# Masked-key copies and a transposed-x copy from ScalarE to VectorE in the prologue of an attention and mixer block

## The chip, the cores and the metric

The kernel runs on one core of one Trainium2 chip. The metric is device time in microseconds (us). A core has five engines that work side by side, each through its own list of instructions in order: TensorE (PE in the profile; its weight loads are PEld), VectorE (DVE), ScalarE (ACT), GpSimd (POOL) and SyncE (SP, which here only starts DMA transfers). They wait for each other by semaphores. Matmul results go to PSUM, eight banks of 128 partitions x 512 fp32 numbers; VectorE and ScalarE copy them from there into SBUF, where the kernel has one tensor, `arena`, for everything.

## The reference

x is 2048 rows of 640 numbers. Two branches start from its layernorm and are multiplied at the end.

```python
def _A_ref(x, wqkv, wo):                       # 32 heads of 20 numbers
    qkv = (x @ wqkv).reshape(B, S, 3, H, Dh).transpose(2, 0, 3, 1, 4)
    q, k, v = qkv[0], qkv[1], qkv[2]
    p = softmax(einsum("bhqd,bhkd->bhqk", q, k) * Dh ** -0.5)
    o = einsum("bhqk,bhkd->bhqd", p, v)
    return o.transpose(0, 2, 1, 3).reshape(B, S, D) @ wo

def _B_ref(x, w1, w2, w3, w4):
    h = gelu(layernorm(x) @ w1)
    # the four quarters of h are moved by +1, -1, +2, -2 rows: g0..g3
    x1 = x + concatenate([g0, g1, g2, g3], -1) @ w2
    return x1 + gelu(layernorm(x1) @ w3) @ w4

xn = layernorm(x)
out = x + _A_ref(xn, A_wqkv, A_wo) * silu(_B_ref(xn, B_w1, B_w2, B_w3, B_w4))
```

## The kernel before

**The work.** The 32 heads are taken in 8 groups of four (quads), and each quad in 4 chunks of 512 queries. For one chunk, 16 tiles of 128 keys are multiplied with the queries: these are the scores. ScalarE takes their exponential, 1024 columns at a time (L1692; 2048 in L1669); for some tiles VectorE does it with integer arithmetic (L1715, then L1602, or L1600 on GpSimd). TensorE multiplies the result with the values (L1432, L1614) and adds it up in bank 7. The other seven banks are a pool that scores and projections share. The mixer and MLP branch and the projections of later quads are worked on between the score tiles.

**Two forms of matmul.** Nearly all matmuls stand in groups of four that use four column strips of the array at once (L733 for projections, L1079 for transposes). Scores can use the four row strips instead (L1623), one strip for each head; a score whose neighbours on TensorE are in column form is done in column form too (L1640). Each change between the two forms takes TensorE some time.

**The prologue.** x is loaded (L920), then the weights of queries and keys of quad 0 (L1102) and of the values (L1341). Layernorm runs tile by tile. TensorE transposes x (L1079) for three of the four column blocks g (the second but one, g = 2, goes by DMA); for each block 5 tiles, numbered `bk` = 0 to 14, are copied out of PSUM, on ScalarE (L1087) where `bk` is in the list `TRA`, on VectorE (L1090) otherwise. `prep` then makes queries and keys of quad 0:

- for each chunk c the key projection (L733) goes to a bank, VectorE takes its largest absolute value (L1217, `mx_c`), and the keys are copied out with a mask and a constant, `mask * k + eaug` (L1220, `kev_c`, on ScalarE);
- the four maxima give a bound of the scores (L1232, L1234), by which the queries of each chunk are shifted: their own copy is L1156, the shift L1165 on TensorE and L1171 on VectorE;
- the first four key tiles start early with a bound from chunk 0 alone (L1186, L1192, L1196), and L1204 and L1208 (`fe`) make the factor by which their sum is corrected later (L1408).

Scores of key tiles 4c to 4c+3 need `kev_c`. A bank comes free when its copy has ended.

**What sets the order.** The functions only record tasks: engine, what is read and written, which bank pool. The string `TABLE` holds the order of all tasks and the bank that each takes; `Planner.follow` reads it and adds the waits that data and banks need. So each engine's order is written out, and nothing is decided at run time. `AGAIN` lists scores that are multiplied more than once (quad, chunk, key tile, head: how many times more), with the same result.

Of the kernel before, what the change touches and what calls it, by code (L numbers as in the profile page):

```python
# [457 lines left out]
U8 = mybir.dt.uint8  # L458
# [19 lines left out]
class Cfg:  # L478
# [5 lines left out]
    def __init__(self, S=2048, D=640, H=32, F=1536):  # L484
# [61 lines left out]
        self.TRA = [1, 2, 4, 5, 6, 7, 8, 9, 13, 16]  # L546
# [110 lines left out]
class Gen:  # L657
# [447 lines left out]
    def prep(self):  # L1105
# [104 lines left out]
        for c in range(NQC):  # L1210
            if c == 1:
# [7 lines left out]
                   reads=[wa], writes=[A("MXc", c)], name=f"mx_{c}", due=self.at(0, "mx", 1, "mxs", c))  # L1219
            T("act", c_act(512) + 100, lambda e, h=h, c=c: e.activation(KT[:, 0, 512 * c:512 * c + 512], self.wbank(h)[:, 0:512], AF.Identity,  # L1220
# [921 lines left out]
    r"#6#9#%#,###(#-#$#&#'#.#e#w&R#l$S#)#*#+#2#Z#f#g$K#[#n$L#]#^$J#h#`#m#c#_#/&S#:#;#<#=#>#?#@#A#B#C#D#E#F#G#H#I#J#K#L#M$M#i#o#p#j#q$'#k${##N#O#P#Q%$$#R#S$q&#T$N#r"  # L2142
    r"$O#s#{$`#x$P#|#y#t$Q#}#z$T$U$V$R$W#b$|#a#d%%&Q#v#~#u$}%&%'$X$##U$l($m$n$v%$r$s$t$w$x$y$~#V$o#W#X#Y$8$)%($u$($z$a$Y$$$*$Z%#$p%g$%`#%a$,$[$]$+$^$_$6#5$-$4%n$%$"
    r"D$5$&$.$/%p$9%b%c$b%h%i%j%8'%k&j&%d&k%9%:%)%&[)&]%l%e$:&^&_%*&`%+%;%3($7$2$3&a$A%<%4%5%6%,&l%=#%>%?&m%.)&T'%7%/$C%@&n%f%0%q$;%1&U&V&c(&W%-&d&e&f&X%2%A&g%r%%t"
    r"#&w)%C$0$@&o$B%u%v%w&x&y&Y$c$E%s$1$<$?$F$>&h&z%m&{*?#$d*<)&|*;(*@$*A%%x'(($G')*='%B'*$e$='+',&6)&7*9#*8$$f$I$g*:&$h'-&8&9&}($H*5(*4)&~*6(%E%D&:'#**#*+$'$'%$i"
    r"$j%U%$k*,$%y%F$%V%G%H%W%o&;%K)%z(H*>%L'&%M%P(%Q%N%I%Z&%O%[%X%R%]%^%{'%|%S%J%}*C)%T%Y*B(%_*2&*1'%~&#(I&&(&'&(&)&<&*'d*D)*-(*3&&$&+*.)*/'&-#0';&'<'=&.'>'?&H#&I"
    r"&2)&J&K(G(J&/&L*7*0&,'@&3&%*]&*^%*_$*J$*K#*H(&M*I)*L&&?#&@&A&B*M&C&4(&5*Q$*P#+#)+$(&D+%'*N&*O'*E'/('0*S'1'2*F'3*U#*V$*R)&q$&=%&r(P&s*W#*X&'4*Y%&>&t&u*f$&v+/("
    r"*Z%+.'*g#*T'I$'J*`%'e#4*G+P(L(K+0(*i*a&'K'L'M''*[*}#'N*|$*m(*l)*o*b&&p*j&*k'&i'5(*~)'6'7'8'9*n#':+1$+2#+3%*c+&+?&*d)&E*r+@'*e('B('C'D'E'F'U&'V'W*h&'X'Y+9$'G+"
    r"A'+8%+:)#7+*(++)+4'O#'P'Q'R'S'.'A&N'H*p+,%*{*x+5%+6&+T$'Z+S#+7#'T*t']#+')*u+((+V'^'_'`'a+Z%+F$+G#+Y&+)&*s'b+;+H(+]+C''c+D(&F$+-+R#+i&+h%+E#+Q$*z+U%&G,#)+~(&O"
    r"#*y+k+I,%#,$)+o&+n%&P+q+t,&$*q'f#+W(+X),'#'g'h+<#+=$,@%,A&'i+[('j'l$'m'k*v+>$*w+B,B&+`(+_',2#,3$+J,5+a$,~'n+c%+b&'o+^&Z'p+l'+d'+m(,(,1#,0$'q+K,9&+p%,8%'r$,;'"  # L2150
    r"s+f'+g('t,4#'u,=#,>$,6&+j)+z,7%'v2d+e,?('w'x#'y+},N(,M),E#,D$'z'{+w'|,P,:$,k%,l&+v,T(,F),S),H#,G$'},<(M#,m%,e&,V'~'[,d%(N,I'+r,C-1(,f$-0',g#,h$,i&,J+s-2)+x+u"
    r",X-&&(#&0-%%,r#,,),s$+|+y,j,-(,t#+{-(,W,Q%,R&,],)#,*$(%#(&('(((),.',+$,^,n(,U&-,#-+$,Y(O,o),p(,[(*,/,v',u&,w$(+((,(--.-:(-9),K#,L$+L,O'(.,q(Q-$&-#'-'%,`+M(/-"
# [128 lines left out]
```

## Time and profile before

| | us |
|---|---|
| runs | 789.10, 789.43, 791.61 |
| median | 789.43 |
| profiled execution, its own time | 788.74 |
| span of the profiled execution (first to last instruction) | 787.0 |
| ScalarE busy in the span | 765.8 |
| TensorE busy, as modelled | 772.6 |
| VectorE busy | 682.0 |
| GpSimd busy | 440.1 |

The granted TensorE clock was 0.999 over the span. Times in the views count from the first instruction. In a group's line stand the source line, the engine, the operation, what it writes and reads, how often, then its busy time and the mean of one in ns, and the idle time of its engine just before with what ended most of it. In a timeline a row is its start, its length, and equal instructions merged; the bracket is the idle time in front and what ended it. `x28` for TensorE is 28 instructions, that is 7 groups of four. Matmuls are pipelined, so a matmul's row is longer than the time from one to the next.

### The profile page before, as it was taken

The page shows a single profiled execution, that of the slowest core. Times are in us where ns is not written, and L with a number is a line of the kernel's source. Part 1 is how long each engine was busy: PE and PEld are TensorE (multiplying, and loading weights), DVE is VectorE, ACT ScalarE, POOL GpSimd, SP SyncE. Part 2 cuts the span into 40 slices and gives each one's busy share as a digit, 9 for nine tenths or more (in the row PEclk, how much of TensorE's full clock was granted, in tenths as well). Part 3 has the DMA queues.
Part 4 walks back from the last instruction along what each step waited for, and adds up shares of the span by engine and source line. Part 5 has one row for each costly group of instructions (what it writes and reads, how often), then busy time and mean ns, then how long its engine had stood idle before and what let it go on. Part 6 is the DMA issues. An engine that isn't in the chain of part 4 may idle for free.

```text
span 787.0 us, 27583 instructions
## 1 busy us (share of the span) xinstructions
PE 772.6 (98%) x12412; PEld 289.8 (37%) x12412; DVE 682.0 (87%) x906; ACT 765.8 (97%) x803; POOL 440.1 (56%) x238
## 2 busy tenths in 40 slices
PE   9999999999999999999999999999999999999997
PEld 5433323324444322333423333323334333332554
DVE  8888888988899989987988889888989879896886
ACT  7999999999999999999999999999999999999996
POOL 6575656553457546666555654676444455636742
PEclk9999999999999999999999999999999999999999
DMA  6403542342122223443221161233341113113443
GB/s 176 88 15 84 136 130 70 88 106 45 14 63 53 49 63 70 98 75 69 53 69 53 36 119 37 61 79 62 73 107 44 19 36 92 21 17 102 134 134 109
DMA packets 141349, 58.09 MB, mean 74 GB/s; under 512 B 113728, under 2 KB 136432, under 8 KB 141232
## 3 DMA queue, kind: packets, MB, share of 16 engines
q1 hardware_dynamic: 141232, 56.33, 31.0%
q8 instruction: 97, 1.59, 0.8%
q14 instruction: 20, 0.16, 0.1%
HBM read 34.70 MB, written 10.33 MB: 57 GB/s over the span
## 4 chain that ended last, share of the span: by engine, by line
PE 51%; ACT 47%; DVE 1%; issue 0%
ACT arena L1692 40%; PE psum L733 19%; PE psum L1623 15%; PE psum L1614 8%; PE psum L1432 6%; ACT arena L2098 3%; PE psum L907 1%; ACT arena L1669 1%; ACT arena L2006 1%; PE psum L1640 1%; ACT arena L2126 1%; PE psum L1489 1%; ACT L1692 0%; DVE arena L1715 0%; PE psum L1463 0%; PE psum L1079 0%
## 5 line engine op out<-in xcount | busy, mean ns | idle before, releaser
L1692 ACT ACTIVATE arena<-psum 128x1024 bf16<-128x1024 f32 x730 | 678.6, 1092 | 10.0 <-PE psum L1623 6.1
L1600 POOL TENSOR_TENSOR arena<-arena 128x2048 int32<-128x2048 int32 x92 | 330.2, 3599 | 198.3 <-DVE arena L1602 122.5
L1715 DVE TENSOR_SCALAR arena<-psum 128x1024 uint16<-128x1024 f32 x264 | 321.4, 1220 | 61.0 <-PE psum L1623 57.0
L733 PE MATMUL psum<-arena 128*32 128x320 bf16 (+1 forms) x5808 | 330.6, 333 | 0.1
L1623 PE MATMUL psum<-arena 32*128 32x512 bf16 x1930 | 257.1, 384 | 5.5 <-ACT arena L1692 3.0
L1614 PE MATMUL psum<-arena 128*22 128x512 bf16 x2112 | 182.0, 381 | 0.0
L733 PEld LDWEIGHTS psum<-arena 128*32 128x32 bf16 x5808 | 134.2, 96 | 122.5 <-issue 52.7
L1623 PEld LDWEIGHTS psum<-arena 32*128 32x128 bf16 x1930 | 69.7, 91 | 232.2 <-ACT arena L1692 151.7
L1432 PE MATMUL psum<-arena 128*22 128x512 bf16 x1456 | 139.2, 382 | 0.6 <-ACT arena L1692 0.5
L1602 DVE TENSOR_SCALAR arena<-arena 128x4096 uint16<-128x4096 uint16 (+1 forms) x121 | 130.1, 1089 | 4.2 <-PE psum L1614 3.4
L1749 POOL TENSOR_TENSOR arena<-arena 128x512 bf16<-128x512 f32 x30 | 40.6, 1355 | 52.0 <-DVE arena L1602 40.5
L1614 PEld LDWEIGHTS psum<-arena 128*22 128x22 bf16 x2112 | 46.9, 90 | 57.6 <-issue 38.6
L1432 PEld LDWEIGHTS psum<-arena 128*22 128x22 bf16 x1456 | 35.1, 90 | 47.7 <-issue 32.0
L2091 DVE CAST arena<-psum 128x512 bf16<-128x512 f32 x48 | 32.6, 683 | 5.0 <-PE psum L733 4.9
L1299 DVE CAST arena<-psum 128x512 bf16<-128x512 f32 x40 | 27.2, 683 | 3.9 <-PE psum L733 3.7
L1914 POOL TENSOR_TENSOR arena<-arena 128x640 bf16<-128x640 bf16 x12 | 16.7, 1398 | 20.7 <-DVE arena L1848 7.9
L1640 PE MATMUL psum<-arena 128*32 128x512 bf16 x272 | 26.8, 382 | 0.1
L1669 ACT ACTIVATE arena<-psum 128x2048 bf16<-128x2048 f32 x13 | 25.3, 1944 | 0.6 <-PE psum L1623 0.5
L944 DVE BATCH_NORM_STATS2 arena<-arena 128x6 f32<-128x320 bf16 x54 | 24.5, 477 | 1.4 <-DMA arena<-in_A_x_dram 1.2
L1848 DVE SCALAR_TENSOR_TENSOR arena<-psum,arena 128x320 bf16<-128x320 f32 x32 | 15.5, 488 | 8.5 <-PE psum L733 8.1
L1736 DVE STREAM_TRANSPOSE arena<-psum 128x512 f32<-128x512 f32 x30 | 21.2, 707 | 1.2 <-PE psum L1432 0.5
L961 POOL TENSOR_SCALAR arena<-arena 128x640 bf16<-128x640 bf16 x16 | 14.0, 876 | 14.5 <-DVE arena L1602 13.3
(135 smaller groups left out, 336.0 us busy)
## 6 DMA issues: line engine op xcount, KB each, us to landing
arena<-in_B_w_dram SPq DMA_DIRECT2D x48, 160.0 KB, 2.7
arena<-arena SPq DMA_DIRECT2D x124, 32.0 KB, 1.9
arena<-in_B_w_dram SPq DMA_DIRECT2D x4, 960.0 KB, 5.8
arena<-in_A_x_dram SPq DMA_DIRECT2D x8, 320.0 KB, 5.4
arena<-in_A_x_dram SPq DMA_DIRECT2D x16, 160.0 KB, 2.6
out_dram<-arena SPq DMA_DIRECT2D x16, 160.0 KB, 2.1
heads<-arena SPq DMA_DIRECT2D x120, 20.0 KB, 2.0
arena<-keys SPq DMA_DIRECT2D x28, 80.0 KB
```

The source lines that it names most:

```text
L733: ins = e.matmul(pb[32 * c:32 * c + 32, 0:N], lhsT(k, c), rhs(k, c), start=(k == 0), stop=(stop and k == nk - 1), tile_position=(0, 32 * c))
L1432: ins = e.matmul(pb[32 * i:32 * i + 22, 0:512], VA[:, ql, kts[i // 2], i, :], PT[:, slots[i // 2][0].slot, slots[i // 2][0].at(i % 2):slot ...
L1600: return e.tensor_tensor(dst.bitcast(I32), U[:, ub, 0:w].bitcast(I32), bass.AP(c.tensor, c.offset, [list(c.ap[0]), [0, w // 2]]), op=ALU.add)
L1602: fa if onp else lambda e, v=v, dst=dst: e.tensor_scalar(dst, U[:, ub, 0:w], EXP_B[v], None, op0=ALU.add),
L1614: ins = e.matmul(pb[32 * i:32 * i + 22, 0:512], wv, dst[:, at:at + 512].bitcast(BF16), start=first, stop=final, tile_position=(0, 32 * i))
L1623: return e.matmul(out, self.KT[32 * i:32 * i + 32, b, 128 * kt:128 * kt + 128], q, start=True, stop=True, tile_position=(32 * i, 0))
L1640: ins = e.matmul(out[32 * c:32 * c + 32, :], self.KT[:, b, 128 * kt + 32 * c:128 * kt + 32 * c + 32], self.QM[:, gb, i, :], start=True, st ...
L1669: lambda e: e.activation(self.PT[:, hp[0].slot:hp[0].slot + 2, :], self.psum[:, 512 * h0.slot:512 * h0.slot + 2048].rearrange("p (a b) -> ...
L1692: lambda e: e.activation(self.PT[:, hp.slot, :].rearrange("p (a b) -> p a b", b=512), self.banks(hs), AF.Exp, scale=cfg.scale),
L1715: return e.tensor_scalar(U[:, ub, 1024 * at:1024 * at + 1024].rearrange("p (a b) -> p a b", b=512), self.banks(hd), a_exp, EXP_BIAS, op0=A ...
L1749: return e.tensor_tensor(OnT.rearrange("p (k d a) -> p a k d", k=4, a=4), Ob[:, :].rearrange("p (a k d) -> p a k d", a=4, k=4), in1, op=AL ...
L2091: T("dve", c_dve(512), lambda e, h=h, fc=fc, i=i, G=G: e.tensor_copy(G[:, i, fc, :], self.wbank(h)[:, 0:512]), reads=[wa], writes=at, name ...
```

## The change

Chunks 1, 2 and 3 of the masked keys are copied by VectorE, in one `tensor_scalar` from the same bank with the same two numbers per partition. Two entries leave `TRA`: 13, the tile of block 3 with kc = 3, which VectorE then copies (L1090), and 16. `AGAIN` is a different list of about the same length. `TABLE` is new as a whole: order and banks were searched again for this set of tasks. The set itself is the same otherwise.

```diff
-        self.TRA = [1, 2, 4, 5, 6, 7, 8, 9, 13, 16]
+        self.TRA = [1, 2, 4, 5, 6, 7, 8, 9]
...
-        self.AGAIN = {(3, 3, 14, 2): 1, (7, 1, 5, 0): 1, (7, 1, 6, 0): 1, (7, 1, 7, 0): 3, (7, 1, 9, 0): 1, (7, 1, 9, 1): 1, (7, 1, 12, 0): 1, (7, 2, 6, 2): 1, (7, 2, 6, 3): 4}
+        self.AGAIN = {(2, 0, 4, 0): 1, (7, 1, 0, 3): 1, (7, 1, 4, 2): 3, (7, 1, 6, 1): 1, (7, 1, 9, 1): 1, (7, 1, 12, 0): 4, (7, 1, 14, 1): 1, (7, 1, 15, 0): 1, (7, 1, 15, 1): 1, (7, 2, 6, 2): 1}
         self.EARLY = 4
+        self.KD = (1, 2, 3)
...
             t1 = T("dve", c_dve(512), lambda e, h=h, c=c: e.tensor_reduce(MXc[:, c:c + 1], ...), ..., name=f"mx_{c}")
+            if c in cfg.KD:
+                T("dve", c_dve(512), lambda e, h=h, c=c: e.tensor_scalar(KT[:, 0, 512 * c:512 * c + 512], self.wbank(h)[:, 0:512], mask[:, 0:1],
+                                                                         self.eaug[:, 0:1], op0=ALU.mult, op1=ALU.add),
+                  reads=[wa, A("eaug"), A("maskh"), A("MXc", c)], writes=at, name=f"kev_{c}", rel=h)
+                continue
             T("act", c_act(512) + 100, lambda e, h=h, c=c: e.activation(KT[:, 0, 512 * c:512 * c + 512], self.wbank(h)[:, 0:512], AF.Identity,
                                                                         bias=self.eaug[:, 0:1], scale=mask[:, 0:1]), ..., name=f"kev_{c}", rel=h)
...
 TABLE = ( ... )    # every line differs
```

On the queues, the first loads now go x (six of eight), query weights, x, x, value weights, key weights; before they went x (five), key weights, x (three), query weights, value weights. Of the 782 tasks that stay on ScalarE, 713 keep their place in its order.

More of the change, by code (lines that the diff above doesn't have):

```diff
@@ L2145 @@
[L2145 to L2152, printed above, removed]
@@ new lines @@
+    r"%$6$@$.$a$^$_%e%3$$/$8$A%='%)#%*%+%,%-%>%?%@%4%5%A%8&%9%:%.%$5%/%0%1%;&c(&d%6&j#&k&e%2%<%f$2$9$7%l%7$3$:$0%q$;$1$C$`&f$4$<&T'&U&V&g$B&h$?&l&W&X%r&&m&n&[$&w%&"
+    r"x&y&Y&]%s&o$E$>&z&{&^&6(&_&`&7$F&a&|$G$b%m*@#$c$d%C$=%B%E%D(P$e*;'*?$*A%*<&$f$H&8&9&:%t$'(%%u%v')'*'+*4$$g*5#(H&;$h%w%x',$I$i%y'-%z*=&*6)*9&$j$k*8%&}#*+$**#*"
+    r":$&~'#'$'%'&%K(%L%Z)%[%M%U%%V%F$%G%H%W%]*,#&<&p#5%^&Z%X%N%_%Y%P#%Q%I%R%S%{&%O%J%|%}%~&#*B&*C%%T';$&&%&'%p#0&(&)&*&H#(G%o'<'='>'?*.$&$&%(I&+&-*D'*1&'@&.*2%*-#"
+    r"*>&I&2$*3(&J&K*/$&L*7&,'d&3*I&*H%*^#*K(&M*]$*J)&?#&@*L)&A&B*M&C*_(&4)*Q(*P)+#%+$$*0*E&5*O&&D*N'*S+%&'/&'0*U$*X(*R#*F*Y)*V%'1'2'3'.''&=)&q#&r&s&t&u'4&>*T*W%*Z"
@@ new lines @@
+    r"'+.#+/$&v+0#*f&*g%*i*a'*`(*[*b%'I$'J'K'L'M(J&/*}$*|#*l%'N*m&*~)*j(*k''5$'6*n$*G'7'8'9+2#*o+1$':+&'B(*e&&E+?)+3'*d'+@('C'D'E'F'U&'V&N'W'X'Y*r'G+4+9$+A&*h)+8%+"
+    r"*(++)*c'O#'P'Q+:''e&i#4'H*x'A*u'R'S*p*{'Z+,%+6$+5#'T+P+S%+T&+V']#'^+')+((+7(+)$'_'`'a*t+G$+F#+H#'b+Y&+Z%+]*s&F#+C)+D(+E)(K+-&G*q+h#+R&+i$#7+k+Q%+;&O#&P,#(+~)"
+    r"+U%,$'+I*y+n%+o&,%#,&$,'$*z'f#+q+t+X(+W)'g+[('h+<#+=$,@%,A&'c'i*v2d'j*w+z+>)'l$,B#'m'k+B+_(+`',3#,2$+J,5'n+a)+b&+c%+d&'o'p+^+m'+l(,1$,0#,9%,8&+p%'q'r$'s+e+g'"
+    r",;+f(+r,4('t+j),~(L+K,=#,7%,6&,>$'u'v+},?&'x#'y'z,E(+L'w,N#,M$,D),('{'|,P,:%,k%'},l&,F),H(,S#,T$,V(Q'~,G),m$+w+M&0,<+v,I'+s,d',h%,e&+|+u,C,g$,J,f%-1#,r)-&&,s"
@@ new lines @@
+    r"(-%'+x(#-(,i&,t',X+y-0$-2),j(M(,,(,-)+{(N,Q',Y,],R&,.&,*%,)$,W(%&(&('(((),+#,Z-,(,o$(*-+),n%,/,U(,^,u&,v'(+&(,(-,p%,w#-.,K$-:(-9),L%,q(.-#&-$''[+N-<(/,O&,x-@"
+    r"%-?$,`(O.K-'%->)-=(,[,c-Y&(Y-A$(0-Z'-B,_,a-[#,b-*)-)(--(-7$-8#(1((2(7#-E(3(4(5-K-4(-3)(8,y-/-;&(6-a$-`#-W&-c-V%-H(9(:-5'-X%-o)-n(-p((;-N(<-R%-f#-g$-S&-i-6-C-"
+    r"T$-e(-d)(Z#([-h&-k&-l%-m)-|#-{$(](^(_-s)/u-r(-t'-~-G-](`(v(=(S&-O$(o-P%.%'.&&-u(#8(R-Q#(h-v).((T(U-F-L-U-w%-^$.|'-_%.}&-b$(V(W-I.+-J-q.~#-y(.$%-z).#$(>(X&1(@"
+    r"..-x($-})-M-j+O(a.''(w&(x(y(z.5&({.,.*,z,{(?((A.4.8$(|.1.6%.9#.:).-(B-D.;%.?).O&.@(.A$.N'.Q.0.7.<$0-&(}0./v.=%0/.C).B(.U&.T'.W.D'0001.S$.R%./.>.M(.L).d&.c'02"
@@ new lines @@
+    r".E.V(.2.Z$.P%.Y%/w&.).f.3.](.[).^).i&.j'/x/y.h%.g$(C.F.l._&.k'/z/{/|.b(.a).`.X.y$/.%.z#/-&/}#.e$/~/'(/()/0.{)0#0$/%#/)&/<&/$$/;%0%/#0'$.o0&0(0)0*0+/=(/2%/1&/"
+    r"`'/_(.m.x,|,}/&)/*(~&/5#)#0,)$/,$/+%04)%/3&/a$/4'/8(//&/9)/:'.q/6.p/@$/?%)&.G/7/b()'/O&/A%/N'/c)/d)/>.r.u.s/C#/B$(b((c(F(E03/Q/D#(d/F)/I&/G(/H'/e/J'(e/M#/K05"
+    r"/L$(f(g/E/P)/i)/j(/l'/S/T/k(.v/f$/^.t/g#06$0708090:/m(/W.n.w/n&0;(D3u3x#3y$4(&.H/Z2e&b4'%40)/Y41(/X/V3{43/h/U4##4)%3~$4*&4+%4,$0<#/o3})3|(4$)0=0>0?4%0@45#0A4"
+    r"4$47%46&4.(4/)42'/R4948#/[/]0B#0C/p0D3v(3w)4<4J%4I&4K(3z&0E0F4?/q0H&5L)(.I0I4E0J4P%4Q$0K0L4-4c&4R#0G)K4b'4d$0M4V)4W(4&4T$4Y4U#(p((q(r4]&4e(4f)4X)4g&4^'4;(s4o"
@@ new lines @@
+    r"#)/)D4p$.J(t4A4`4i)(u4l&4k'4j(4=4>4h4s%5%$5&%4n4m'4q)5'$4r(4Z&4B4N#4['4@4t5$4_&4:4M$)>()?)@50(4G&4w4z)=4O%5/)4F'4D)A)B4S4C4a5(#5)$51'4H#5<(5;)4v5*)4u53&)C5>5"
+    r"4'))(4L)*55$56#57&5,(5-))+),59&5:')-5+585.#5O)5M$5P(4}5N#4x52).5=(0N5~&5Q$5}'5R/r5Z%4y4{5_#5V)5^$6#%5U(5@5`'5F4~5[&5#4|5X5A5z#5{$5](5T'5D5d(5B5e)5?(i(5S&5E(j"
+    r"9t5|)5g5C(k5b#5c$5G5k(5j)5W&62&63'5f#(l6$(m5Y5m5h$5i#66%/s6%(5l$(n5p6&)0Q5n)E#)F)G)H0V6@&6)#6($6')6A%)I0O5y5o0P$0R5a6*&6/()J69#6:$0S6.'6B$5r6+6;')L$6,%6-&)M)"
+    r"N65#6160#64$6='6<()O)P)6Da6N&6M%5q676>)5s5v5u6I'6G$6J()Q6H#6Q&6L686?6j&6K(6k%)0$)16l)6C#6O'6P(6D$)2)3)46E'6g%6R6h&6i#)55t5w5H6`$6d'6a#6c(6F6e%6U6_5x6v6X)7$6b"
@@ new lines @@
+    r"$6m)86n#)9):);)<6o'6f6S6}$6~#6W6[/t)R7%)0U6V)S$6x%6z'6y(6w&)T)U)V)W)Y)o5I0T8G6|)X76#75$6{&7R%7Q&7$(7#'6p6Y6T79#7/)71#72$)a)}6]6Z5J7&70(6^7S%)Z()[747g&73'7f'7"
+    r"8#7h(6q77$7:7@)]7V)7U()^)_7'7W&7Y$7O#7N$)`7X'7d)7P)7c(7F)b()c7Z7_$7['7^#7a7e&7]&7`#)d)e7m(7n)7o')f)h)v)g7T8.&8-'7s$8/)7t#7b7B80(81))i()j7k'7j&82#7l%)k)l7v88#"
+    r"84)87$85(7A83)m7p7;7i89$7=7r'7y#86))n8?&7z$8>%7|7?7>7q()p$)q)r8@&7w&7x%7u#8<#8;$)s)t8:8=')~#*#)u7C8#7{)7D7+(7H#7G$7,)6r7I(8&7E*$7-$*%Di))w()x)y*&)z*'){7<Dj8Q"
+    r"(8P)8`$8_#Du#)|DvDwDxDyDk8b8SDlDm5K7~Dc&Do(DzDd8K(8J)8f$DpDq2cDeDfDnDgDr8MDs6s*(3,#3-*)3.3/30Dh2f)2g2h2i2j8%2kDt318e#8'8,2{%8(7(%2m#2n2o2p8$8h7)&2t$2q2u2v2w0"
```

178 lines of the change are left out of this document (81 added, 97 removed).

## The prediction

> **What bounds the kernel now.** I read the page first: the engines' busy time, the chain that ended last, the costliest group.
>
> ```profile
> PE 772.6 (98%) x12412; PEld 289.8 (37%) x12412; DVE 682.0 (87%) x906; ACT 765.8 (97%) x803; POOL 440.1 (56%) x238
> PE 51%; ACT 47%; DVE 1%; issue 0%
> L1692 ACT ACTIVATE arena<-psum 128x1024 bf16<-128x1024 f32 x730 | 678.6, 1092 | 10.0 <-PE psum L1623 6.1
> ```
>
> ScalarE (ACT) is busy 97% of the span, nearly all of it the exponential of scores, and it sat idle before those for only 10.0 us. The chain, however, goes half through TensorE (PE). So it matters which of the two leads in the stage that the change touches. The second view is busy time by stage; the columns are the window, its length, then busy time and count of PE, PEld, DVE, ACT, POOL.
>
> ```profile
> 21.40:35.00 13.60, 13.60 (x292) 6.16 (x284) 11.56 (x29) 12.55 (x15) 7.56 (x9) 1.00 0.59 108
> 35.00:80.00 45.00, 45.00 (x653) 15.19 (x651) 39.15 (x48) 44.99 (x50) 30.43 (x24) 1.00 0.20 51
> 80.00:140.00 60.00, 59.98 (x815) 17.96 (x811) 52.66 (x60) 58.56 (x63) 35.93 (x15) 1.00 0.43 107
> 140.00:200.00 60.00, 59.41 (x943) 22.11 (x944) 52.37 (x63) 59.42 (x56) 28.76 (x12) 1.00 0.33 80
> 200.00:260.00 60.00, 59.86 (x1054) 25.33 (x1050) 55.40 (x82) 58.34 (x63) 31.18 (x14) 1.00 0.21 41
> 520.00:720.00 200.00, 197.41 (x3018) 70.55 (x3009) 170.79 (x187) 199.89 (x205) 108.27 (x38) 1.00 0.26 54
> ```
>
> From 35 to 80 us ScalarE is idle for 0.01 us: there it sets the pace. Just before, from 21.4 to 35 us, it is idle for 13.60 - 12.55 = 1.05 us. That is the stretch of the moved copies; ScalarE's timeline shows it.
>
> ```profile
> 21.39 4.69 ACT L1692 ACTIVATE arena<-psum 128x1024 bf16<-128x1024 f32 x5
> 25.94 0.80 ACT L1220 ACTIVATE arena<-psum,arena 128x512 bf16<-128x512 f32 x1
> 26.60 0.63 ACT L1087 ACTIVATE arena<-psum 128x512 bf16<-128x512 bf16 x1
> 27.77 2.98 ACT L1692 ACTIVATE arena<-psum 128x1024 bf16<-128x1024 f32 x3 [0.54 <-PE psum L1623]
> 30.64 1.44 ACT L1220 ACTIVATE arena<-psum,arena 128x512 bf16<-128x512 f32 x2
> 32.56 1.94 ACT L1692 ACTIVATE arena<-psum 128x1024 bf16<-128x1024 f32 x2 [0.48 <-PE psum L1623]
> 34.39 0.60 ACT L1208 ACTIVATE arena<-psum 128x512 f32<-128x512 f32 x1
> 35.01 5.61 ACT L1692 ACTIVATE arena<-psum 128x1024 bf16<-128x1024 f32 x6
> ```
>
> After each pair of copies ScalarE waits for TensorE's scores, 0.54 and 0.48 us. The copies stand in time that ScalarE has anyway. The chain of waits, asked for 21 to 36 us, agrees: no piece of it is on ScalarE or VectorE.
>
> ```profile
> by line: PE psum L733 59.9%; PE psum L1623 22.0%; PE psum L1079 7.9%; PE psum L1432 6.5%; PE psum L1204 2.9%; PE psum L1165 1.4%
> 27.71 1.62 PE psum L733 x28
> 31.74 0.43 PE psum L1432 x8
> 32.17 0.54 PE psum L1623 x6
> 32.71 1.19 PE psum L733 x20
> ```
>
> These rows also price TensorE's work. 28 matmuls are 7 groups of four, 20 are 5: (1.62 - 1.19) / 2 = 0.215 us for a group of 512 columns, and 1.62 - 7 x 0.215 = 0.11 us is left for the switch between row-form scores and the column form of everything else. Six scores in two passes take 0.11 + 2 x 0.215 = 0.54 us, as shown.
>
> **The change part by part.** (1) What leaves ScalarE. TRA lists tiles of transposed x by number, and only 15 exist, 0 to 14; entry 16 never named one. So one copy of x (tile 13) moves and not two, with three of keys: four instructions. In the rows above they hold ScalarE from 25.94 to 27.23 and from 30.64 to 32.08: 1.29 + 1.44 = 2.73 us. That is the most that can be gained here.
>
> (2) What TensorE must do before the first exponential after the copies' stretch (35.01 us). I counted the orders of the two built programs up to that exponential's scores: the same instructions stand there, but for one group of L1432, which goes behind. That frees 0.215 us. All else (projections, transposes, scores) is still ahead, and TensorE has no gap there. So of 2.73 us ScalarE can hand on about 0.2; the rest becomes its idle time.
>
> (3) What VectorE (DVE) gets, in its timeline:
>
> ```profile
> 26.36 1.62 DVE L1090 COPY arena<-psum 128x512 bf16<-128x512 bf16 x4 [0.48 <-PE psum L1079]
> 29.39 0.69 DVE L1217 TENSOR_REDUCE arena<-psum 128x1 f32<-128x512 f32 x1 [0.39 <-PE psum L733]
> 30.31 0.23 DVE L1234 TENSOR_SCALAR arena<-arena 128x4 bf16<-128x4 f32 x1
> 31.15 0.75 DVE L1171 SCALAR_TENSOR_TENSOR arena<-psum,arena 128x512 bf16<-128x512 f32 x1 [0.16 <-PE psum L1165]
> 31.82 0.74 DVE L1156 TENSOR_SCALAR arena<-psum,arena 128x512 bf16<-128x512 f32 x1
> ```
>
> A masked key copy has the form of L1156, and from start to start the rows 31.15 and 31.82 give 0.67 us; a copy of x is 1.62 / 4 = 0.41. Added: 3 x 0.67 + 0.41 = 2.42 us. VectorE's idle time from 21.4 to 35 us is 13.60 - 11.56 = 2.04, so it is over-full by 0.4 us unless small work leaves. The new order puts the copy of keys 2 ahead of the third maximum (L1217), and that of keys 3 behind L1234 but ahead of L1171. Queued behind the latter are the shifted queries (L1171), for which the next scores on TensorE wait, and behind those TensorE's whole queue. The fifth copy of x stands ahead of the last key projection. Bounds: nothing, if the gaps take it all (0.48 + 0.39 + 0.16 are shown above), and 2.42 us if none do. I take 0.3, near the excess over the idle time; less than nothing is excluded, since VectorE loses no work.
>
> [...]
>
> (4) What is moved on the queue of SyncE (SP). Before, the key weights (first L1102) are the sixth load, the query weights the tenth, the value weights (L1341) the last. In the new order the query weights are seventh, the value weights tenth and the key weights last. The views are SP's timeline, and the two lines with their times to landing (L1102, then L1341):
>
> ```profile
> 3.35 0.47 SPq L1102 DMA_DIRECT2D arena<-in_A_wqkv_dram  x1
> 5.53 1.27 SPq L1102 DMA_DIRECT2D arena<-in_A_wqkv_dram  x1
> 6.84 1.64 SPq L1341 DMA_DIRECT2D arena<-in_A_wqkv_dram  x1
> DMA to landing us min/median/max: 5.6/6.1/6.6
> DMA to landing us min/median/max: 3.3/5.2/7.2
> 12.87 1.91 PE psum L733 x32
> ```
>
> Key weights landed at 3.35 + 5.6 = 9.0 us, query weights at 5.53 + 6.6 = 12.1, and the last load at 6.84 + 7.2 = 14.0. TensorE's first projections began at 12.87 (last row, from the chain of waits). With the same loads in another order the last still lands at about 14.0, and now it is the keys'. TensorE starts with three query groups, 3 x 0.215, and stands at its first key group at 13.5: it waits about 0.5 us, with everything behind it in its queue. Bounds: nothing (landed by 13.5) and, if this load is issued when L1341 ended (8.5) and takes 6.6, 15.1 - 13.5 = 1.6. I take 0.5. On GpSimd's (POOL) queue the small value copies move ahead of two memsets; POOL is busy 7.56 of 13.60 us here, which covers them, and I cost them at nothing; without that cover each is under 1 us on a queue that no exponential waits for here.
>
> (5) The order behind the prologue. ScalarE's order hardly changes; TensorE's is re-sorted. In the built orders the stretches of row-form scores go from 557 to 552 (10 switches fewer, -1.1 us), passes inside them from 662 to 668 (+1.3), column-form scores from 68 to 75 (+1.5), repeated scores from 14 to 15 (within these): TensorE gets 1.7 us more in all. By place it is 0.6 to 1.1 us less than after the prologue up to about 400 us, and 1.5 to 3 us more from about 510 to 715. In the first part ScalarE's idle time from 80 to 260 us is 1.44 + 0.58 + 1.66 = 3.7 us, and less TensorE work can shorten it by 1.1 at most. In the second there is cover:
>
> ```profile
> PEld psum L1623 <- ACT arena L1692: 42.6, 114, 0.8
> ```
>
> That is the waits from 520 to 720 us: TensorE waits 42.6 us there for ScalarE, so 3 us more hide. Bounds -1.1 and +1.7; I take -0.5.
>
> Sum: -0.2 + 0.3 + 0.5 - 0.5 = +0.1 us. The profiled execution took 788.74 us (span 787.0, 1.7 around it), which becomes 788.8; the median of the runs is 0.7 higher, 789.43, and my number is for that: **789.5 us**.
>
> **The rivals.** A (faster): ScalarE's 2.73 us come through whole, 786.7 us. For it: ScalarE leads from 35 us on, so whatever it gains before is kept to the end; and the banks that it frees sooner let TensorE's scores start earlier. Against it: the waits of 0.54 and 0.48 us and the chain. It needs TensorE to put scores ahead of projections, which the counted order does for one group only. [...]
>
> B (slower): VectorE becomes the bound of the prologue. Place: key copies 2 and 3 ahead of L1171, and the fifth x copy ahead of the last key projection. Price: all 2.42 us, in which no gap helps because each gap was a wait for TensorE, which now itself waits for VectorE; 789.43 + 2.42 = 791.9. It decides once VectorE's idle time there (2.04) is used up. For it: 2.42 is more than 2.04. Against it: those 2.04 us are gaps between the very instructions that the copies are put among.
>
> C: the 1.7 us of TensorE's later work find no cover: 791.1. Against it: the 42.6 us of waits.
>
> **How the numbers follow.** A measurement of this kernel can tell about 0.3%, 2.4 us, from no change. Forecast 0.52, C 0.06: both within it, 0.58. A 0.20, just over 0.3% faster. B 0.22, just over 0.3% slower. The forecast's own bounds go from -0.2 - 1.1 = -1.3 to -0.2 + 2.42 + 1.6 + 1.7 = +5.5, of which I count only the part up to B. The forecast's own range is 788.1 to 791.1. To leave out no more than 2 in 10 the range reaches to A and B: 786.7 to 792.0.
>
> **What would show it.** Right: ScalarE's first exponential not earlier than 21.3 us and its pass after L1204's (35.01 now) between 34.8 and 36; ScalarE idle there up by some 2.5 us; a wait of TensorE near 13.5 us with a DMA as its releaser; VectorE nearly without gaps from 24 to 34 us; ScalarE's idle time from 80 to 260 us under 3.7. Wrong towards A: that pass at 32.5 us with ScalarE never idle. Wrong towards B: TensorE waiting for L1171, L1090 or the new key copy by more than 2 us in all. If the prologue comes out as said but the time differs by over 2 us, step (5) was wrong.

## The result and the profile after

| | us |
|---|---|
| changed kernel, median of 15 runs | 791.59 (790.93 to 791.98) |
| kernel before, 15 runs | 789.48 (788.47 to 791.61) |
| ratio, 95% interval | 1.0026 (1.0019 to 1.0033) |
| span of the profiled execution, after (before) | 789.2 (787.0) |

The changed kernel is 2.1 us slower. The forecast was 789.5, so the sum was 2 us short. The time lies inside the range of 786.7 to 792.0, near its slow end, and outside the forecast's own range of 788.1 to 791.1.

In the changed source L733 became L734, L1079 L1080, L1087 L1088, L1090 L1091, L1156 L1157, L1171 L1172, L1204 L1205, L1208 L1209, L1217 L1218, L1220 L1226, L1361 (VectorE's copies of the values) L1367, L1432 L1438, L1614 L1620, L1623 L1629, L1640 L1646, L1692 L1698 and L1715 L1721. The new key copy is L1222; L1956 is a small VectorE operation of the layernorm. All experiments below use this numbering.

Page of the changed kernel: busy time, the chain that ended last by engine, the costliest group.

```profile
PE 773.1 (98%) x12434; PEld 292.8 (37%) x12434; DVE 683.6 (87%) x910; ACT 763.9 (97%) x799; POOL 439.3 (56%) x238
PE 62%; ACT 32%; DVE 5%; issue 0%
L1698 ACT ACTIVATE arena<-psum 128x1024 bf16<-128x1024 f32 x730 | 678.7, 1081 | 14.0 <-PE psum L1629 11.3
```

ScalarE has four instructions and 1.9 us less to do, but it idles 14.0 us before its exponentials, not 10.0; 11.3 us of that is for scores (L1629), where it was 6.1. The chain went to TensorE, 62% after 51%. Busy time by stage of the changed kernel, with the columns of before:

```profile
21.40:35.00 13.60, 13.46 (x290) 6.07 (x278) 13.02 (x31) 9.83 (x11) 8.32 (x14) 1.00 0.53 105
35.00:80.00 45.00, 44.62 (x660) 15.30 (x659) 39.30 (x48) 45.00 (x50) 30.48 (x20) 1.00 0.23 56
80.00:140.00 60.00, 59.81 (x826) 18.22 (x822) 52.18 (x60) 58.44 (x63) 34.63 (x15) 1.00 0.42 104
140.00:200.00 60.00, 59.53 (x951) 22.06 (x947) 51.89 (x63) 59.44 (x56) 28.55 (x11) 1.00 0.35 81
200.00:260.00 60.00, 59.48 (x1040) 24.92 (x1028) 55.07 (x84) 58.38 (x63) 31.53 (x14) 1.00 0.19 40
520.00:720.00 200.00, 197.47 (x3024) 71.18 (x3024) 171.80 (x188) 199.29 (x203) 106.78 (x37) 1.00 0.26 56
```

In the stretch of the copies ScalarE is busy for 9.83 us, not 12.55: all 2.72 us that left it became idle time. VectorE is busy for 13.02 of 13.60. From 520 to 720 us ScalarE now idles 0.71 us, where it idled 0.11. ScalarE's timeline shows the first part:

```profile
21.22 4.97 ACT L1698 ACTIVATE arena<-psum 128x1024 bf16<-128x1024 f32 x5
28.11 1.02 ACT L1698 ACTIVATE arena<-psum 128x1024 bf16<-128x1024 f32 x1 [1.92 <-PE psum L1629]
30.58 1.94 ACT L1698 ACTIVATE arena<-psum 128x1024 bf16<-128x1024 f32 x2 [1.45 <-PE psum L1629]
32.80 1.94 ACT L1698 ACTIVATE arena<-psum 128x1024 bf16<-128x1024 f32 x2 [0.29 <-PE psum L1629]
34.75 0.60 ACT L1209 ACTIVATE arena<-psum 128x512 f32<-128x512 f32 x1
35.24 1.02 ACT L1698 ACTIVATE arena<-psum 128x1024 bf16<-128x1024 f32 x1
```

Three waits of 1.92, 1.45 and 0.29 us, and the pass after L1209 stands at 35.24 us, 0.23 later than before. So 2 us more are lost behind the prologue. To see where, I took the start of the same pass (same scores) in both traces and subtracted. The column of before has the start itself; the others tell how many us later the pass starts than there. Most of the experiments run the order of one kernel up to a seam and that of the other behind it; three of their columns stand here too.

| pass of ScalarE | before | after | front_only | rest_only | end_only |
|---|---|---|---|---|---|
| first exponential | 21.39 | -0.17 | 0.05 | 0.04 | 0.07 |
| after the factor | 35.01 | 0.23 | 0.42 | 0.04 | 0.07 |
| quad 1, chunk 1 | 148.80 | 0.51 | 0.59 | 0.21 | 0.07 |
| quad 3, chunk 0 | 324.02 | 1.10 | 0.68 | 0.80 | 0.07 |
| quad 5, chunk 1 | 515.38 | 1.22 | 0.78 | 0.92 | 0.06 |
| quad 6, chunk 1 | 638.96 | 1.76 | 0.83 | 1.45 | 0.59 |
| quad 7, chunk 1 | 714.16 | 2.22 | 0.88 | 1.91 | 1.05 |
| last instruction | 782.78 | 2.19 | 0.91 | 1.87 | 1.02 |

I call this the ledger. Where a column runs the order of before it should stay level, and does so within 0.02 us in end_only up to its seam; front_only drifts by 0.3 us over the 630 us after 148.80. So steps are read here, not drifts. The steps themselves come again where the same order runs: the one near 611 us is 0.55 us in after, rest_only and end_only alike. Each column is one execution, so a step that a late load causes is in it too. The first row goes with when loads land: the key weights landed at 13.6 us in after and at 13.87 in front_only.

### The profile page after: what moved, and what is told of

Read it like the earlier page. It is cut to its first block, busy times and chain, and to the rows that moved or that the text cites. A ratio compares the mean times of both kernels' runs of the same rounds, so it can differ in the third digit from the quotient of the medians.

```text
span 789.2 us, 27635 instructions
## 1 busy us (share of the span) xinstructions
PE 773.1 (98%) x12434; PEld 292.8 (37%) x12434; DVE 683.6 (87%) x910; ACT 763.9 (97%) x799; POOL 439.3 (56%) x238
## 4 chain that ended last, share of the span: by engine, by line
PE 62%; ACT 32%; DVE 5%; issue 0%
ACT arena L1698 29%; PE psum L734 22%; PE psum L1629 18%; PE psum L1620 10%; PE psum L1438 7%; DVE arena L1721 2%; PE psum L1646 1%; PE psum L908 1%; ACT arena L2012 1%; ACT arena L1675 1%; PE psum L1495 1%; PE psum L1469 0%; ACT arena L2132 0%; PE psum L1080 0%; DVE arena L1305 0%
## 5 line engine op out<-in xcount | busy, mean ns | idle before, releaser
L1698 ACT ACTIVATE arena<-psum 128x1024 bf16<-128x1024 f32 x730 | 678.7, 1081 | 14.0 <-PE psum L1629 11.3
L1721 DVE TENSOR_SCALAR arena<-psum 128x1024 uint16<-128x1024 f32 x264 | 321.1, 1220 | 65.9 <-PE psum L1629 61.6
L734 PE MATMUL psum<-arena 128*32 128x320 bf16 (+1 forms) x5808 | 329.4, 333 | 0.3
L1629 PE MATMUL psum<-arena 32*128 32x512 bf16 x1924 | 256.6, 384 | 7.3 <-ACT arena L1698 3.9
L1620 PE MATMUL psum<-arena 128*22 128x512 bf16 x2112 | 184.5, 381 | 0.0
L734 PEld LDWEIGHTS psum<-arena 128*32 128x32 bf16 x5808 | 137.2, 96 | 120.3 <-issue 51.6
L1629 PEld LDWEIGHTS psum<-arena 32*128 32x128 bf16 x1924 | 69.6, 91 | 231.3 <-ACT arena L1698 148.4
L1438 PE MATMUL psum<-arena 128*22 128x512 bf16 x1456 | 140.1, 382 | 0.3 <-ACT arena L1698 0.2
L1620 PEld LDWEIGHTS psum<-arena 128*22 128x22 bf16 x2112 | 47.2, 90 | 62.2 <-issue 42.5
L1438 PEld LDWEIGHTS psum<-arena 128*22 128x22 bf16 x1456 | 35.4, 90 | 47.1 <-issue 28.3
L1646 PE MATMUL psum<-arena 128*32 128x512 bf16 x300 | 29.4, 381 | 0.1
L1742 DVE STREAM_TRANSPOSE arena<-psum 128x512 f32<-128x512 f32 x30 | 21.3, 710 | 1.6 <-PE psum L1438 0.7
```

Source lines behind the costliest of these rows:

```text
L734: ins = e.matmul(pb[32 * c:32 * c + 32, 0:N], lhsT(k, c), rhs(k, c), start=(k == 0), stop=(stop and k == nk - 1), tile_position=(0, 32 * c))
L1438: ins = e.matmul(pb[32 * i:32 * i + 22, 0:512], VA[:, ql, kts[i // 2], i, :], PT[:, slots[i // 2][0].slot, slots[i // 2][0].at(i % 2):slot ...
L1620: ins = e.matmul(pb[32 * i:32 * i + 22, 0:512], wv, dst[:, at:at + 512].bitcast(BF16), start=first, stop=final, tile_position=(0, 32 * i))
L1629: return e.matmul(out, self.KT[32 * i:32 * i + 32, b, 128 * kt:128 * kt + 128], q, start=True, stop=True, tile_position=(32 * i, 0))
L1646: ins = e.matmul(out[32 * c:32 * c + 32, :], self.KT[:, b, 128 * kt + 32 * c:128 * kt + 32 * c + 32], self.QM[:, gb, i, :], start=True, st ...
L1698: lambda e: e.activation(self.PT[:, hp.slot, :].rearrange("p (a b) -> p a b", b=512), self.banks(hs), AF.Exp, scale=cfg.scale),
```

## The experiments

A seam is a place in the order at which both kernels have done exactly the same tasks. At two of them, after 800 and after 4690 of the 6675 tasks, the banks held are the same as well, so the order can change over there.

**Which part of the order costs the time: front_only, rest_only, end_only.**

```diff
 front_only
-TABLE = after
+TABLE = after[:800] + before[800:]      # AGAIN of before
 rest_only
-TABLE = before
+TABLE = before[:800] + after[800:]      # AGAIN of after, copies on ScalarE
 end_only
+TABLE = before[:4690] + after[4690:]    # AGAIN of each part, copies on ScalarE
```

> The changed kernel's first 800 tasks (to about 96 us of the span: prologue, the four moved copies, quad 0 up to chunk 2), then the order, banks and repeated scores of the kernel before. At this seam the same tasks are done and the same banks held in both. Theory 1, the cost is in the later order: the passes of ScalarE at 96 us are 0.33 us late in the profile of the changed kernel, and nothing is added after that: 789.48 + 0.33 = 789.8 us. Theory 2, the moved copies and their order cost the time, by what they set off later: 791.4 us or more, about as much as the whole change.

> The reverse: the first 800 tasks of the kernel before, with the four copies on ScalarE, and the changed kernel's order, banks and repeated scores from there on. Theory 1: of the 2.19 us by which ScalarE's last instruction is late, 2.19 - 0.33 = 1.86 us come after this seam: 789.48 + 1.86 = 791.3 us. Theory 2: 789.5 us, as before.

> The kernel before up to the second seam (task 4690, about 518 us), the changed kernel's order from there on. Theory 1: the ledger of ScalarE's passes is 1.22 us late at this place and 2.19 at the end, so this part costs 1.0 us: 790.5 us. That it hides because TensorE waits 42.6 us there for ScalarE (the prediction's step 5): 789.5 us. If all of the later cost were here: 791.3 us.

| | us | before | ratio, 95% interval |
|---|---|---|---|
| front_only | 790.08 | 789.13 | 1.0014 (1.0005 to 1.0023) |
| rest_only | 790.96 | 789.13 | 1.0027 (1.0017 to 1.0037) |
| end_only | 789.93 | 789.13 | 1.0012 (1.0003 to 1.0020) |

Each run stands beside runs of the kernel before that were taken with it. Both parts cost: 0.95 us by the front, 1.83 by the rest, about half of the latter behind 518 us: 0.80 in end_only (interval 0.2 to 1.6), so that part does not hide. Theory 2 falls, since the rest costs its 1.8 us with the copies on ScalarE as they were. Theory 1 holds for the rest (1.83, expected 1.86) and was too low for the front (0.95, expected 0.33). The two together are more than the whole (2.1), within their intervals.

**Why the front costs more than the changed kernel's own trace said: front_keys_early.** The chain of waits of front_only begins with a load:

```profile
7.26 6.61 DMA arena<-in_A_wqkv_dram
13.87 0.04 issue
13.91 1.70 PE psum L734 x28
...
34.94 0.60 ACT arena L1209
```

These are the key weights, last on SP's queue. They landed at 13.87 us, and the projection (L734) starts with them. In the changed kernel's own profile TensorE's weight loads wait for them too, but less:

```profile
13.65 0.40 PEld L734 LDWEIGHTS psum<-arena 128*32 128x32 bf16 x12 [0.28 <-DMA arena<-in_A_wqkv_dram]
```

```diff
-SP: x0 x2 x4 x6 x8 x10 query_weights x14 x12 value_weights key_weights
+SP: x0 x2 x4 x6 x8 x10 query_weights key_weights x14 x12 value_weights
```

> As front_only, with one entry of the order moved: the load of the key weights stands right behind that of the query weights (8th load of SP), not last. In front_only the chain of waits goes through this load (landed 13.87 us), and TensorE's weight loads wait 0.6 us for it (0.28 us in the changed kernel's own profile). If step 4 of the prediction is right, and the rest of the prologue follows: ScalarE's pass after L1209's at 34.8 to 35.1 us and not 35.43, 789.7 us, 0.3 to 0.5 under front_only. If VectorE's chain from 26.5 to 32.5 us holds the pace whatever comes before it, or the two tiles of x that now load later take as much: 790.1 us, as front_only.

789.12 us beside 789.32, ratio 0.9996 (0.9988 to 1.0005). The front's loss against the kernel before is gone within the error, 1.0 us under front_only and more than the 0.3 to 0.5 that I expected. So in the timed runs the load's place is the larger part of the front's cost.

The traces show less of it. The pass after L1209 stands at 35.24 us, neither within 34.8 to 35.1 nor at 35.43. Of front_only's 0.91 us at the end of the ledger 0.54 are gone, but only 0.2 of that stands there by this pass; the rest comes in pieces under 0.1 us, where both run the same order. And the changed kernel's own pass is at 35.24 us too, with this load still last. Its chain of waits there holds the same pieces of VectorE as front_keys_early, at the same times to 0.02 us. At that pass, then, the late load cost nothing where it landed at 13.6 us and 0.2 where it landed at 13.87. The timed runs may hold later landings, but no trace here shows where the rest of their 1.0 us comes from.

**VectorE's chain against TensorE's work: front_mix.**

```diff
-TRA = [1, 2, 4, 5, 6, 7, 8, 9];      KD = (1, 2, 3)
+TRA = [1, 2, 4, 5, 6, 7, 8, 9, 13];  KD = (1, 3)
```

> As front_only, with two of the four copies back on ScalarE, where it idles 1.92 and 1.44 us in front_only: keys 2 and the tile of x (the copies of keys 1 and 3 stay on VectorE). VectorE's chain loses 0.71 + 0.41 = 1.1 us. If that chain holds the prologue (rival B's mechanism): the pass after L1209's at 34.3 us, and 789.0 us, 1.1 under front_only. If TensorE's work is the floor (the forecast; 35.01 - 0.2 = 34.8 us in the kernel before, 0.2 to 0.4 more here for the late key weights): 35.0 to 35.2 us, 789.8 us. If ScalarE can't take them without delay to its exponentials: 790.5 us or more.

790.22 us beside 789.32, ratio 1.0014 (1.0005 to 1.0022): as front_only. The chains of waits say why. First that of the changed kernel, in the stretch that carries the copies:

```profile
26.33 1.75 DVE arena L1091 x5
28.08 0.61 DVE arena L1218
28.69 0.03 issue
28.71 0.81 DVE arena L1222
29.52 0.08 DVE arena L1956
29.60 0.60 DVE arena L1218
...
30.93 0.70 DVE arena L1222
31.63 0.67 DVE arena L1172
```

There VectorE holds the pace from 26.3 to 32.3 us, with two key copies and the fifth x copy in it. In front_mix no piece of the chain up to L1209 is on VectorE; it is TensorE's:

```profile
14.31 0.04 issue
14.35 1.70 PE psum L734 x28
...
28.66 2.09 PE psum L734 x44
...
34.90 0.46 PE psum L1205 x8
35.37 0.02 issue
35.39 0.60 ACT arena L1209
```

From the first L734 piece to L1209 front_mix takes 35.39 - 14.35 = 21.04 us and front_only 34.94 - 13.91 = 21.03. Taking 1.1 us out of VectorE's chain gives nothing, because TensorE's work stands right under it. The pass after L1209 is at 35.88 us, 0.45 later than in front_only, and the landing accounts for that: 14.31 and not 13.87 us. It is later than the 35.0 to 35.2 that I expected of TensorE's work as the floor, by more than the landing alone.

**The copies on VectorE in the old order: before_on_dve.**

```diff
-TRA = [1, 2, 4, 5, 6, 7, 8, 9, 13];  KD = ()
+TRA = [1, 2, 4, 5, 6, 7, 8, 9];      KD = (1, 2, 3)    # TABLE and AGAIN of before
```

> The order, banks and repeated scores of the kernel before, with nothing changed but the engine of the four copies: they go to VectorE, at the places that the old order gives them there. Forecast (gaps of VectorE and ScalarE's room cancel): 789.1 to 789.7 us, at most 0.6 over the kernel before. Rival B (VectorE over-full, each copy delays TensorE): 791.5 us. Rival A (2.73 us of ScalarE come through): 786.4 us.

791.38 us beside 789.32, ratio 1.0025 (1.0016 to 1.0034), which is rival B. The pass after L1209 is 2.42 us late, the price that the prediction put on B; that it agrees to the hundredth is chance, since the pieces of the chain add up otherwise. Its chain of waits:

```profile
24.65 0.75 DVE arena L1157
25.40 0.72 DVE arena L1222
...
32.00 0.71 DVE arena L1222
32.71 0.40 DVE arena L1367
33.10 0.66 DVE arena L1172
33.76 0.72 DVE arena L1222
34.48 0.67 DVE arena L1157
35.15 0.04 issue
35.19 1.26 PE psum L734 x20
```

Here all three key copies lie in the chain, the third between two copies of queries. TensorE's projections (L734, 35.19) wait for the second of these, by its bank.

**The copies on ScalarE in the new order: front_on_act.**

```diff
-TRA = [1, 2, 4, 5, 6, 7, 8, 9];      KD = (1, 2, 3)
+TRA = [1, 2, 4, 5, 6, 7, 8, 9, 13];  KD = ()           # TABLE of front_only
```

> As front_only, but the four copies stay on ScalarE, at the places that the new order gives them. Tells what the move itself is worth in one and the same order. The forecast's reading, TensorE's work is the floor and either engine has room: 789.8 us, within 0.4 of front_only, and ScalarE's pass after L1209's at 34.8 to 35.6 us. If the 2.73 us of copies weigh fully on ScalarE: 792.2 us. If VectorE's new chain (copies of keys 2 and 3, 0.70 us each in the chain of waits of the changed kernel, and 0.41 of x) holds the prologue: 1.8 us faster than front_only, 788.0 us.

794.80 us beside 789.13, ratio 1.0072 (1.0059 to 1.0084), worse than every expectation. ScalarE's timeline:

```profile
21.79 1.00 ACT L1698 ACTIVATE arena<-psum 128x1024 bf16<-128x1024 f32 x1
25.08 0.78 ACT L1226 ACTIVATE arena<-psum,arena 128x512 bf16<-128x512 f32 x1 [2.28 <-DVE arena L1218]
25.75 3.75 ACT L1698 ACTIVATE arena<-psum 128x1024 bf16<-128x1024 f32 x4
31.09 0.60 ACT L1088 ACTIVATE arena<-psum 128x512 bf16<-128x512 bf16 x1 [1.58 <-PE psum L1080]
34.48 0.78 ACT L1226 ACTIVATE arena<-psum,arena 128x512 bf16<-128x512 f32 x1 [2.79 <-DVE arena L1218]
```

The order that was made for VectorE puts the copy of keys 1 right behind ScalarE's first exponential, and four exponentials queue behind it while it waits 2.28 us. So this run prices a bad place, not the engine, and doesn't tell what the move is worth. TensorE was then busy for 1.61 us only from 24 to 28 us, and its granted clock was 0.50 from 28 to 32 us. That adds to the loss: in the chain of waits the 80 transposes (L1080) and five groups of projections behind 29.54 us take 2.13 + 2.02 us, where front_mix, with the same order, has 1.22 + 1.09.

**Is the later cost local: end_shift and end_swap.** The ledger of end_only grows by 0.5 us near 611 us. In names, sc6_0_8_0 are the scores of quad 6, chunk 0, key tile 8, first two heads; s0_4_1 is a projection in five groups.

```diff
 end_shift
-s0_4_1 (5 groups) ... sc6_1_3_0 ... sc6_0_8_0 ... sc6_0_1_1 ... sc6_1_2_1 ... sc6_0_13_0
+sc6_1_3_0 ... sc6_0_8_0 ... sc6_0_1_1 ... sc6_1_2_1 ... sc6_0_13_0 ... s0_4_1 (5 groups)
 end_swap
-sc6_1_3_0 [banks 0, 1]  sc6_0_8_0 [6, 5]  ...  sc6_1_2_1 [1, 0]  sc6_0_13_0 [5, 6]
+sc6_0_8_0 [0, 1]  sc6_1_3_0 [6, 5]  ...  sc6_0_13_0 [1, 0]  sc6_1_2_1 [5, 6]
```

> As end_only, with one edit in the order at about 610 us: the five groups of one projection (s0_4_1, 5 x 0.215 = 1.08 us of TensorE) go behind eight score tiles that they stood among. There the least work of TensorE ahead of a pass rises from 1.9 to 2.9 us over the kernel before, and ScalarE waits 0.55 us at that very pass. If the later cost is local (work of TensorE put ahead of scores that ScalarE needs next): 0.3 to 0.55 us of end_only's 1.02 in the ledger goes, 789.5 us. If the cost comes from the amount of TensorE's work, wherever it stands: nothing goes, 789.9 to 790.1 us.

> As end_only, with the order and banks of four tiles exchanged at 611 us. There the new order puts the scores of VectorE's next tile (sc6_1_3_0) ahead of those of ScalarE's next pass (sc6_0_8_0), and gives the latter the banks that VectorE's exponential frees at 611.63 us, not those that ScalarE's own pass freed at 610.81. Here sc6_0_8_0 goes first with the banks of sc6_1_3_0, and the reverse; and so with the next pair, sc6_0_13_0 and sc6_1_2_1. TensorE's work is the same. If step 5 went wrong by such local places (which scores stand first, and whose release they wait for): 0.3 to 0.5 us of end_only's 1.02 in the ledger goes at this place, and ScalarE no longer waits there (0.42 us in end_only): 789.6 us. If it is the amount of TensorE's work: nothing goes, 790.1 us.

end_shift: 793.47 us beside 789.32, ratio 1.0051 (1.0038 to 1.0064). It says nothing on the question, as the edit was incomplete: the copy of the projection out of its bank kept its place on VectorE, VectorE waited 2.8 us for it, and the next tiles and that bank waited behind. The granted clock was 0.83 from 610 to 620 us on top of it.

end_swap: 790.43 us beside 789.03, ratio 1.0018 (1.0009 to 1.0027), so nothing was gained over end_only. ScalarE's timeline in end_only:

```profile
609.77 1.95 ACT L1698 ACTIVATE arena<-psum 128x1024 bf16<-128x1024 f32 x2
612.14 23.10 ACT L1698 ACTIVATE arena<-psum 128x1024 bf16<-128x1024 f32 x25 [0.42 <-PE psum L1629]
```

The same timeline in end_swap:

```profile
609.98 2.96 ACT L1698 ACTIVATE arena<-psum 128x1024 bf16<-128x1024 f32 x3
613.22 1.94 ACT L1698 ACTIVATE arena<-psum 128x1024 bf16<-128x1024 f32 x2 [0.28 <-PE psum L1629]
615.38 20.41 ACT L1698 ACTIVATE arena<-psum 128x1024 bf16<-128x1024 f32 x22 [0.23 <-PE psum L1629]
```

The wait of 0.42 us did go, as the edit meant. But 0.28 and 0.23 us came back at passes one and three places later. From 515 to 639 us the ledger grows by 0.53 us in end_only and by 0.88 in end_swap. (A step of 0.42 us near 466 us in end_swap, ahead of its edit, comes with a wait for a load and is not part of this.)

So this exchange moves the waits and does not remove them. My reading is that the amount of TensorE's work decides how much waiting there is; that is not shown. For it: in end_only the chain of waits from 606 to 611.7 us is TensorE's but for 0.70 us, and by the count of the built orders TensorE's least work ahead of a pass rises by 1.06 us over the kernel before within six passes here. Against it: in end_swap the chain runs through two exponentials of VectorE (L1721, 1.23 and 1.24 us, from 610.62 to 613.59), whose tile the edit put behind, so the waits of 0.28 and 0.23 us may come from that. No run here keeps the places and takes the work away.

**The repeated scores: rest_no_repeat and its control, before_no_repeat.**

```diff
-AGAIN = {...}
+AGAIN = {}
```

> As rest_only, with no score multiplied more than once (15 repeats fewer, 14 of them in quad 7; 15 x 0.215 = 3.2 us less work of TensorE at most). The results are the same. If the later cost is TensorE's amount of work near the end (rival C): up to 1 us under rest_only, 790.0 us. If it is made of local waits elsewhere, as the ledger says (0.9 us late at 518 us, 1.5 at 639, before quad 7): 791.0 us, as rest_only. If the repeats bring something by themselves (a clock that stays granted, another form of the neighbouring scores): slower than rest_only.

before_no_repeat, as expected:

> The kernel before with no score multiplied more than once (14 repeats fewer), the control for rest_no_repeat. If repeats are dead weight of TensorE: 789.3 us or up to 1 us under it; if they bring something: over 789.6 us.

rest_no_repeat: 791.29 us beside 789.03, ratio 1.0027 (1.0016 to 1.0037), as rest_only. before_no_repeat: 789.90 us beside 789.03, ratio 1.0010 (1.0001 to 1.0018). Less work made it slower; the last section shows how. The same loss is in rest_no_repeat, 0.98 us of the ledger from 716 to 720 us, so its time alone doesn't clear the repeats. rest_only's ledger does: it stands at 1.77 us at the pass that starts at 711.35 us in the kernel before, ahead of quad 7's repeats, and at 1.83 behind them. Rival C's 1 us isn't in the repeats.

## Why the prediction fell short, step by step

**(1) What leaves ScalarE, 2.73 us.** Right: 2.72 us less busy time in the stretch, four instructions fewer.

**(2) TensorE's work is the floor; ScalarE can hand on 0.2 us.** Right in the mechanism, while the 0.2 us itself can't be told apart in the runs: ScalarE idles 3.66 us in three waits for scores, and front_mix shows TensorE's chain right beneath VectorE's. Rival A, the 2.73 us whole, is out: ScalarE's occupancy of 97% over the span does not name the engine that sets the pace in this stretch.

**(3) VectorE's copies, 0.3 us.** Right for the new order. A key copy holds VectorE for 0.71 to 0.73 us from its start to the next, in the changed kernel's timeline. The 0.67 that was taken is in fact the time of L1171 in the kernel before, from its start (31.15) to that of L1156 (31.82). The chain is VectorE's, but no later than TensorE's would be. With the load mended, the whole front costs -0.2 us in the timing (interval -0.9 to 0.4) and 0.37 in the ledger. In the old order rival B came true, 2.42 us at the pass and 2.1 in the timing. The new order is what takes B's price away.

**(4) The late key weights, 0.5 us, bounds 0 to 1.6.** Right in the mechanism. Forecast was a landing at about 14.0 us; the profiles of after, front_only and front_mix show 13.6, 13.87 and 14.31. The size is open: front_keys_early against front_only gives about 1.0 us in the timed runs, the traces 0 and 0.2 at the pass after L1209, and 0.45 more in front_mix, where the load landed last.

Steps 1 to 4 gave +0.6 us for the front. The changed kernel's trace shows +0.23 at the pass after L1209, front_only 0.42 there and 0.95 in its time. Of the prediction's signs for the prologue two were missed by little: the first exponential came at 21.22 us (not before 21.3 was said), and ScalarE's idle time from 80 to 260 us was 3.74 us (under 3.7 was said). The others came: that pass between 34.8 and 36 us, 2.72 us more of idle time on ScalarE, a wait of TensorE near 13.5 us for a load, VectorE nearly without gaps.

**(5) The order behind the prologue, -0.5 us, bounds -1.1 and +1.7.** This is the term that was mis-sized: rest_only measures +1.83 us (interval 1.3 to 2.9), at its upper bound or over it, and of the other sign than the -0.5 taken. The prediction named the sign of it: the prologue comes out as said, and the time differs by over 2 us (791.59 - 789.5 = 2.1). Two readings in it failed. First, TensorE's 0.6 to 1.1 us less work up to 400 us was to shorten ScalarE's waits. ScalarE's idle time from 80 to 260 us is 1.56 + 0.56 + 1.62 = 3.74 us, as before, and by 515 us rest_only is 0.92 late. Second, TensorE's added work from 510 us on was to hide in 42.6 us of waits for ScalarE, which was also the case against rival C. The view of the waits from 520 to 720 us, after:

```profile
PEld psum L1629 <- ACT arena L1698: 42.6, 113, 0.7
```

The waits are still there, all 42.6 us, and 1 us was lost beside them. So a sum over 200 us of waits is no cover for work that is placed in 6 us. Why, is argued and not shown: each of these waits is for a bank that ScalarE still reads, so TensorE can't use it to work ahead, and a burst that grows by 1 us finds only the scores that stand ready in banks at that moment. Rival C had the right size (791.1) for a part of the right reason, and 0.06 was too little for it. B's number, 791.9, lies nearer still to 791.59, but not by its mechanism. It was in part luck that the range held: it was stretched to 792.0 for B, and what filled it was step 5.

What stays open: the 0.9 us that the order from 96 to 518 us costs. The ledger collects them in some dozens of steps of 0.1 to 0.65 us, with gains among them, while TensorE has less work than before up to that place. More than half comes at one place: between the passes that start at 266 and 277 us in the kernel before the ledger grows by 0.52 us, in after and in rest_only alike. There ScalarE waits 0.27 us for scores at 274.38 us (rest_only). In that trace the chain of waits goes through VectorE, an exponential (L1721) and a transposition (L1742) from 267.07 to 268.93 us, where in the kernel before it is all on TensorE. So that part is not TensorE's work alone. Why VectorE comes late there, and where the rest is lost, is not traced.

## What to carry to other kernels

- Where two engines share the pace, work taken off one can become its idle time; first ask what the other engine has in the same stretch. Here 2.72 us taken off ScalarE were worth nothing, and so were 1.1 us taken off VectorE's chain.
- When an order is searched anew for a small change, price the whole new order, with its loads: one load put last cost the front about 1 us in the timed runs, more than four moved copies.
- Don't take an engine's waits over 200 us as cover for work that stands in a few us: here 42.6 us of waits stayed, and 1 us was lost beside them. And compare the start of the same instruction in both traces; this ledger finds a loss of 1 us that no busy share shows.

## What the runs showed of the hardware that I had not expected

Fewer matmuls made the kernel before slower by 0.87 us (interval 0.1 to 1.4). Its busy time without the repeats, in two windows of 4 us (PE, PEld, DVE, ACT, POOL, then the granted clock):

```profile
720.00:724.00 4.00, 2.97 (x29) 0.71 (x28) 2.22 (x2) 3.91 (x5) 2.39 (x1) 0.89 0.99 344
724.00:728.00 4.00, 4.00 (x48) 1.07 (x47) 3.01 (x4) 3.21 (x3) 1.09 (x2) 0.69 0.18 59
```

and two rows of TensorE's timeline in it:

```profile
722.35 0.39 PE L1646 MATMUL psum<-arena 128*32 128x512 bf16 x4
724.94 0.64 PE L1646 MATMUL psum<-arena 128*32 128x512 bf16 x4
```

TensorE is idle for 1.03 of 4 us there, in gaps of at most 0.53 us. The granted clock has a mean of 0.89 over these 4 us and of 0.69 over the next 4, and the row of a group is 0.64 us long and not 0.39. From 716 to 720 and from 728 to 732 us it is 1.00. By my estimate from the two windows, (0.11 + 0.31) x 4 = 1.68 us of the full clock are missing. The ledger of this run stays between 0.2 and 0.4 us up to its pass of 722.8 us, and stands at 1.58 at that of 728.6 and at the end, so the loss is there. It is the same in rest_no_repeat: clock 0.59 from 716 to 720 us, and 0.98 us lost. With the repeats, the kernel before has TensorE busy for 3.67 of the 4 us from 720 to 724, and the clock is 1.00 from 716 to 732; in rest_only it is 1.00 from 712 to 728 us. So in both kernels the clock stayed up with the repeated scores and fell without them, though TensorE was busy for 2.97 of the 4 us in which it fell. How much idle time makes it fall, no run here shows. The repeats are padding here, and who removes them should do it with an eye on that column.
